# Float64 weights unpacked during the first layer and kept, split, in DRAM

## The chip, the cores and the metric

One core of a Trainium2 chip runs the kernel. The metric is device time in microseconds (us), the median over runs. Engines are called as in the profile: PE (TensorE, matmuls), PEld (its weight loads), DVE (VectorE), ACT (ScalarE), POOL (GpSimd), SP (SyncE, whose queue issues nearly all DMAs). L12 is line 12 of the kernel before.

## What is computed

A kernelized attention makes x (1152 tokens by 512). A first layer of four experts (512 to 1024 to 512, ReLU) is summed with token weights, and a second layer follows. Its weights arrive as float64.

```python
x = attention(q, k, v, omega)              # [1152, 512]
for e in range(4):                         # w1 [4, 512, 1024], w2 [4, 1024, 512], float32
    h = np.maximum(x @ w1[e], 0.0)
    out += p[:, e:e+1] * (h @ w2[e])
h = out @ w_in                             # w_in [512, 2048], float64
return ((h * np.cos(h)) @ w_out).astype(np.float32)   # w_out [2048, 512], float64
```

## The kernel before, in words

Every float32 product runs as three float32r products: an operand is split into hi and lo, and hi*hi, hi*lo and lo*hi are added. So each weight is needed as a hi tile and a lo tile.

The dense layers are six "experts": 0 to 3 are the first layer's, 4 and 5 the two halves of the second layer's 2048 hidden units. Each expert passes over three chunks of 384 tokens. A chunk has eight hidden tiles (`hidden`, L174, 12 matmuls each, 128x384), and three output tiles (`gemm2`, L220, 24 matmuls each, 128x512). Two hidden tiles of the next chunk run ahead of a chunk's second product (`gemm1_ahead`), so that on PE the order is 96 matmuls of L174, 72 of L220, 96 of L174, and so on.

The stream of dense work is cut into quanta (one hidden tile, or a third of an output tile); a chunk has 17 and an expert 51. Behind a quantum each side chain under way takes one step (`advance`), and `plan` says behind which quantum a chain starts. The order on each engine is thus the program's order; Tile adds the waits.

Evacuation of a hidden tile: in the first layer `relu_split`, one ACT and one DVE instruction (L230, L231). In the second layer `cos_split`, a chain of seven: ACT cv (L240), DVE ck (L241), POOL cv (L244), ACT ck (L246), DVE cv (L247), ACT hh (L249), DVE hl (L250). PE needs hh and hl of all eight tiles in each output tile, and the last of them near its end.

Weights come in sets (an expert's first or second product) of four units. Set number mod 3 picks one of three sets of buffers in SBUF. `load32` (first layer) takes a DMA, an ACT copy to hi and a DVE subtraction to lo (L96). `load64` (second layer) handles half a unit: a DMA of raw words (L110 or L118), ACT Abs (L122), five DVE instructions (L129, L132, L137, L140, L142), an ACT copy to hi (L145), and two POOL instructions, the subtraction (L147) and the addition of the low word to lo (L148). There are 32 such halves. `plan` starts them in expert 3 (sets 8 and 9) and expert 4 (sets 10 and 11), one expert ahead of their use. All raw tiles, of both kinds, share three buffers.

`second_x` turns the first layer's output back into the second's input: 12 groups of three transposes on PE (L298), four of them during the first chunk of expert 4.

Of the kernel before, what the change touches and what calls it, by code (L numbers as in the profile page):

```python
# [8 lines left out]
F32 = mybir.dt.float32  # L9
F32R = mybir.dt.float32r  # L10
# [5 lines left out]
# float32 products run as three float32r products: every operand is split exactly  # L16
# into hi (its 12 leading bits) and lo (the rest), and
# a*b = a_hi*b_hi + a_hi*b_lo + a_lo*b_hi up to 2**-24 of the product.

INV_2PI = 0.15915494309189535  # L20
TWO_PI_DOWN = 6.283185  # largest float32 whose half does not pass pi
# [4 lines left out]
def performer_moe_kernel(ctx, tc, q, k, v, omega, probs, w1, w2, w_in, w_out, out):  # L26
    nc = tc.nc
# [6 lines left out]
    R = 4  # neighbouring tokens in a partition  # L34
    SB = P * R  # tokens of a batch in whole tiles
    L = S - SB  # tokens of a batch in the shared tile
# [3 lines left out]
    TC = 3  # token tiles of a chunk  # L40
# [4 lines left out]
    EPS = 1e-6 * M  # the features are kept without their 1/sqrt(M)  # L45
# [11 lines left out]
    late = {}  # pools that take the attention's place  # L57
# [5 lines left out]
    # Set 2 * e is expert e's w1, set 2 * e + 1 its w2; the two halves of the second  # L63
    # layer's hidden units go as experts E and E + 1.
# [34 lines left out]
    def load64(st, u, z):  # L99
        """Half z of a unit, as three steps. float64 words are (low, high); the high word's  # L100
        21 bits make the float32 a, and the low word weighs 2**-52 times a's power of two."""
        hf = st // 2 - E
        n = UW // 2
        tmpp = late["tmp"]
        t = tmpp.tile([P, n], U32, tag="f64t", name=f"t{st}_{u}_{z}")
        raw = rawp.tile([P, n, 2], U32, tag="raw", name=f"raw{st}_{u}_{z}")
        lw, hw = raw[:, :, 0], raw[:, :, 1]
        if st % 2 == 0:
            c0 = hf * F + u * 256
            nc.sync.dma_start(  # L110
                out=raw.rearrange("p (k f) t -> p k f t", f=256),
                in_=w_in32[z * 256 : (z + 1) * 256, c0 : c0 + 256, :].rearrange(
                    "(k p) f t -> p k f t", p=P
                ),
            )
        else:
            r0 = hf * F + u * 256 + z * P
            nc.sync.dma_start(out=raw, in_=w_out32[r0 : r0 + P, :, :])  # L118
        yield
        yield  # L120
        # magnitudes below float32's range become 0
        nc.scalar.activation(t.bitcast(F32), hw.bitcast(F32), ACTF.Abs)  # L122
        yield
        if z == 0:
            new_unit(st, u)
        hi, lo = (x[:, z * n : (z + 1) * n] for x in units[st, u])
        a = tmpp.tile([P, n], U32, tag="f64a", name=f"a{st}_{u}_{z}")
        b = tmpp.tile([P, n], F32, tag="f64b", name=f"b{st}_{u}_{z}")
        nc.vector.tensor_scalar(  # L129
            out=t.bitcast(F32), in0=t.bitcast(F32), scalar1=2.0**-15, scalar2=None, op0=ALU.max  # L130
        )
        nc.vector.tensor_scalar(  # L132
            out=a, in0=t, scalar1=0x07FFFFFF, scalar2=3,
            op0=ALU.bitwise_and, op1=ALU.logical_shift_left,
        )
        yield
        nc.vector.scalar_tensor_tensor(  # L137
            out=a, in0=hw, scalar=0xC0000000, in1=a, op0=ALU.bitwise_and, op1=ALU.bitwise_or
        )
        nc.vector.tensor_scalar(out=t, in0=a, scalar1=0xFF800000, scalar2=None, op0=ALU.bitwise_and)  # L140
        yield
        nc.vector.scalar_tensor_tensor(  # L142
            out=b, in0=lw, scalar=2.0**-52, in1=t.bitcast(F32), op0=ALU.mult, op1=ALU.mult
        )
        nc.scalar.activation(hi, a.bitcast(F32), ACTF.Copy)  # L145
        yield
        nc.gpsimd.tensor_tensor(out=a.bitcast(F32), in0=a.bitcast(F32), in1=hi.bitcast(F32), op=ALU.subtract)  # L147
        nc.gpsimd.tensor_tensor(out=lo, in0=a.bitcast(F32), in1=b, op=ALU.add)  # L148
        yield

# [8 lines left out]
    def advance(under):  # L159
        """One step of each chain that is under way, the oldest first."""  # L160
        for g in list(under):
            if next(g, under) is under:
                under.remove(g)

    def hidden(e, c, f):
        """A tile of the hidden layer: [128 units, CW tokens]."""
        xh, xl = x_t[c]
        wh, wl = units[2 * e, f // 2]
        acc_ps = bank(f"g1_{e}_{c}_{f}")[:, :CW]
        n = 0  # L170
        for kk in range(KD):
            o = kk * 256 + (f % 2) * P
            for a, b_ in ((wh, xh), (wh, xl), (wl, xh)):
                nc.tensor.matmul(  # L174
                    acc_ps, a[:, o : o + P], b_[:, kk, :], start=n == 0, stop=n == 3 * KD - 1
                )
                n += 1
        return acc_ps

    heads = {}  # hidden tiles that run ahead, before the last chunk's second product  # L180
# [24 lines left out]
    def gemm2(e, c, evac):  # L205
        last = (e, c) == (E + 1, NCH - 1)
        for j in (2, 0, 1) if last else range(TC):
            # the very last tile in two pieces, so that less is left to do behind it
# [27 lines left out]
    def cos_split(src, hh, hl):  # L236
        vv = late["g"].tile([P, CW], F32, tag="cv", name="cv")
        kk = late["g"].tile([P, CW], F32, tag="ck", name="ck")
        # cos(h) = sin(2 pi (u - round(u))), u = h / (2 pi) + 1/4
# [51 lines left out]
    def second_x(c):  # L291
        """The first layer's output of a chunk as the second one's input, by steps."""
        new_x(c)
        xh, xl = x_t[c]
        for kk in range(KD):
            tp = bank(f"tx2_{c}_{kk}")[:, :CW]
            for j in range(TC):
                nc.tensor.transpose(  # L298
                    tp[:, j * P : (j + 1) * P], acc[c * TC + j][:, kk * P : (kk + 1) * P], ident
                )  # L300
            yield
            nc.scalar.activation(xh[:, kk, :], tp, ACTF.Copy)
            nc.vector.tensor_tensor(
                out=xl[:, kk, :], in0=tp, in1=xh[:, kk, :].bitcast(F32), op=ALU.subtract
            )

    # Expert e in quanta: chunk c begins at 17 * c with 6 of gemm1, 2 of the next chunk's
    # gemm1 and 9 of gemm2. starts[e][q]: what begins behind quantum q.
# [7 lines left out]
    def plan():  # L316
        for st in range(2, 2 * E + 4):
            e, k = st // 2 - 1, st % 2
            for u in range(NU):
                if st < 2 * E:  # L320
                    q = 38 + 3 * u if k else (20 + 4 * u if e == 0 else 3 + 9 * u)
                    start_at(e, q, lambda st=st, u=u: load32(st, u))
                else:
                    for z in range(2):
                        q = 30 + 2 * (2 * u + z) if k else 3 + 3 * (2 * u + z)
                        start_at(e, q, lambda st=st, u=u, z=z: load64(st, u, z))
# [5 lines left out]
    def dense():  # L332
# [3 lines left out]
        for n, (e, c) in enumerate(seq):  # L336
            if c == 0:
                q = 0
            parts = [gemm1(e, c, relu_split if e < E else cos_split)]
# [19 lines left out]
    with tc.tile_pool(name="at1", bufs=1) as at1, tc.tile_pool(name="at2", bufs=2) as at2:  # L359
        # work that wakes the tensor engine's clock while the first loads are under way  # L360
# [7 lines left out]
        # the table of exponentials comes in while the first loads are under way  # L368
# [5 lines left out]
        # values of the shared tile, each batch's rows in columns of their own  # L374
# [31 lines left out]
        # omega transposed, one copy for each half of a pair, the other half's rows zero  # L406
# [19 lines left out]
        def norms(nm, t):  # L426
            """sum((x * SC)**2) / 2 of each row."""
# [10 lines left out]
        def turn(nm, t):  # L438
            """Rows in pairs, transposed; what it returns splits them."""
# [14 lines left out]
        def features(nm, turned, phi):  # L454
            """phi[:, row, :] = exp(h - max(h)), h = SC * proj - sq; in three steps."""
# [18 lines left out]
            # max(h) = SC * max(proj) - sq, then the exponent's bias -sq - max(h)  # L474
# [17 lines left out]
        def divide(nm, parts):  # L492
            """dst = num / (den + eps) for (num, dst) in parts, 4 groups of D + 1 columns each."""
# [13 lines left out]
        def put_x(nm, kk, xs, t0, n):  # L507
            """Token tiles t0 .. t0 + n - 1 of the heads of pair kk into the chunks."""
# [19 lines left out]
        # per pair: [features, head, batch, value and count]  # L528
# [94 lines left out]
        # loads, two pairs ahead  # L623
# [22 lines left out]
        first = 6  # the step from which batch 0 is through  # L646
# [38 lines left out]
        # in the place of the first queries' features, which come after it  # L685
        xkL = at1.tile([P, 2, R * P], F32R, tag="phq", name="xkL")
        turned["kL"] = turn("kL", kL)(xkL[:, 0, :], xkL[:, 1, :])
        for s in range(NPR + 3):
# [14 lines left out]
            if s == 0:  # L703
                # the keys of the tile that both batches share
# [60 lines left out]
    late["tmp"] = ctx.enter_context(tc.tile_pool(name="tmp64", bufs=2))  # L765
    late["g"] = ctx.enter_context(tc.tile_pool(name="gp", bufs=3))
    new_acc(ctx.enter_context(tc.tile_pool(name="acc2", bufs=1)), TC, NTILE)
    for _ in stream:
        pass
# [28 lines left out]
```

## Time and profile before

| | |
|---|---|
| median of 3 runs | 721.22 us (720.83 to 721.45) |
| span of the profiled execution | 719.5 us |
| median less span (what lies around it) | 1.7 us |
| PE busy | 697.3 us, 97% of the span |
| DVE, ACT, POOL busy | 410.2, 250.9, 203.3 us |
| granted TensorE clock, mean | 0.991 |
| moved by DMA | 43.68 MB, mean 61 GB/s |

How to read it: the span is one execution, from first to last instruction. Busy matmuls overlap in the records, so a busy share of PE near 100% says that it never waited long, not that it was at its peak; a stage's length is therefore read from when its first matmul and the next stage's first matmul start.

### The profile page before, as it was taken

The numbers are of one execution on the slowest core, as the hardware profiler recorded it, in microseconds if no ns is written. First come the engines' busy times: TensorE is split into PE (matmuls) and PEld (weight loads), VectorE is DVE, ScalarE is ACT, GpSimd is POOL, SyncE is SP. The second block draws the span as 40 slices with busy tenths as digits, with TensorE's granted clock in tenths as the row PEclk, the third lists the DMA queues.
The fourth block names the chain that finished last, engine by engine and source line by source line (L and its number), as shares of the span: only waits on it lengthen the run. The fifth ranks groups of instructions, "written<-read, shape, count | busy, mean of one in ns | idle before, by whom it ended". The sixth has DMA issues, their size and how long they took to land.

```text
span 719.5 us, 9723 instructions
## 1 busy us (share of the span) xinstructions
PE 697.3 (97%) x3781; PEld 632.3 (88%) x3781; DVE 410.2 (57%) x755; ACT 250.9 (35%) x556; POOL 203.3 (28%) x168
## 2 busy tenths in 40 slices
PE   8999999999999999999999999999997998889998
PEld 8889998989898998989898989999786796769897
DVE  6999753414323232423133488599789889865252
ACT  4776740313121212112031223233645463253240
POOL 6565320000000000000000144345657566644150
PEclk9999999999999999999999999999999898999999
DMA  7554110022200011100022122123021212000001
GB/s 190 179 134 126 38 59 1 30 58 67 81 30 29 31 30 58 59 30 30 29 59 61 57 74 88 51 89 111 29 87 60 88 55 65 27 16 30 21 24 45
DMA packets 37519, 43.68 MB, mean 61 GB/s; under 512 B 13664, under 2 KB 26208, under 8 KB 37472
## 3 DMA queue, kind: packets, MB, share of 16 engines
q1 hardware_dynamic: 37328, 43.02, 20.0%
q8 instruction: 30, 0.49, 0.3%
q14 instruction: 17, 0.14, 0.1%
q10 hardware_dynamic: 144, 0.03, 0.0%
HBM read 40.68 MB, written 2.36 MB: 60 GB/s over the span
## 4 chain that ended last, share of the span: by engine, by line
PE 69%; DVE 20%; ACT 5%; issue 2%; POOL 1%; DMA 1%; SPq 0%; DVEq 0%; ACTq 0%
PE g L174 33%; PE g L220 31%; DVE t L129 3%; DVE a L132 2%; DVE hl L250 2%; DVE a L137 2%; DVE b L142 2%; DVE ck L241 1%; DVE cv L247 1%; ACT phk L487 1%; ACT hh L249 1%; PE num L577 1%; DVE mx_k L471 1%; PE pj_q L467 1%; PE kv L548 1%
## 5 line engine op out<-in xcount | busy, mean ns | idle before, releaser
L230 ACT ACTIVATE hh<-g 128x384 fp32r<-128x384 f32 x96 | 47.2, 493 | 255.7 <-PE g L174 154.0
L147 POOL TENSOR_TENSOR a<-a,w_0h 128x512 f32<-128x512 f32 x8 | 12.5, 1562 | 328.6 <-ACT w_0h L145 318.5
L231 DVE SCALAR_TENSOR_TENSOR hl<-g,hh 128x384 fp32r<-128x384 f32 x96 | 51.8, 554 | 83.3 <-ACT hh L230 83.2
L267 DVE SCALAR_TENSOR_TENSOR acc<-g,pn,acc 128x512 f32<-128x512 f32 x27 | 20.3, 750 | 102.2 <-PE g L220 102.2
L244 POOL TENSOR_TENSOR cv<-cv,ck 128x384 f32<-128x384 f32 x48 | 58.2, 1218 | 62.8 <-DVE ck L241 62.8
L174 PE MATMUL g<-xh,w_0h 128*128 128x384 f32 x144 | 48.9, 340 | 2.9 <-DVE cv L247 2.9
L174 PE MATMUL g<-xh,w_3h 128*128 128x384 f32 x144 | 48.7, 338 | 0.7 <-ACT acc L276 0.7
L220 PE MATMUL g<-w_2h,hl 128*128 128x512 f32 (+1 forms) x110 | 43.5, 396 | 5.9 <-DVE hl L250 5.9
L174 PE MATMUL g<-xh,w_2h 128*128 128x384 f32 x144 | 48.6, 337 | 0.0
L174 PE MATMUL g<-xh,w_1h 128*128 128x384 f32 x144 | 48.4, 336 | 0.0
L174 PE MATMUL g<-xh,w_1l 128*128 128x384 f32 x144 | 48.3, 336 | 0.0
L174 PE MATMUL g<-xl,w_1h 128*128 128x384 f32 x144 | 48.2, 335 | 0.0
L174 PE MATMUL g<-xh,w_3l 128*128 128x384 f32 x144 | 48.2, 335 | 0.0
L174 PE MATMUL g<-xh,w_0l 128*128 128x384 f32 x144 | 48.2, 335 | 0.0
L174 PE MATMUL g<-xl,w_0h 128*128 128x384 f32 x144 | 48.1, 334 | 0.0
L174 PE MATMUL g<-xh,w_2l 128*128 128x384 f32 x144 | 48.1, 334 | 0.0
L174 PE MATMUL g<-xl,w_3h 128*128 128x384 f32 x144 | 48.1, 334 | 0.0
L174 PE MATMUL g<-xl,w_2h 128*128 128x384 f32 x144 | 48.1, 334 | 0.0
L220 PE MATMUL g<-w_3h,hh 128*128 128x512 f32 (+1 forms) x110 | 44.4, 404 | 2.4 <-ACT hh L249 2.4
L220 PE MATMUL g<-w_2h,hh 128*128 128x512 f32 (+1 forms) x110 | 43.1, 392 | 2.1 <-ACT hh L249 2.1
L220 PE MATMUL g<-w_3h,hl 128*128 128x512 f32 (+1 forms) x110 | 43.8, 398 | 0.0
L220 PE MATMUL g<-w_0h,hl 128*128 128x512 f32 (+1 forms) x110 | 43.4, 395 | 0.0
(187 smaller groups left out, 1839.5 us busy)
## 6 DMA issues: line engine op xcount, KB each, us to landing
raw<-in_moe_w_dram SPq DMA_DIRECT2D x32, 512.0 KB, 3.5
raw<-in_moe_w_in_dram SPq DMA_DIRECT2D x16, 512.0 KB, 3.7
raw<-in_moe_w_out_dram SPq DMA_DIRECT2D x16, 512.0 KB, 3.5
kt<-in_k_dram SPq DMA_DIRECT2D x8, 256.0 KB, 2.9
qt<-in_q_dram SPq DMA_DIRECT2D x8, 256.0 KB, 3.2
ve<-in_v_dram SPq DMA_DIRECT2D x16, 128.0 KB, 3.1
out_dram<-acc SPq DMA_DIRECT2D x7, 256.0 KB, 2.3
out_dram<-acc SPq DMA_DIRECT2D x4, 128.0 KB, 2.3
```

The costliest lines, as they stand in the source:

```text
L129: nc.vector.tensor_scalar(out=t.bitcast(F32), in0=t.bitcast(F32), scalar1=2.0**-15, scalar2=None, op0=ALU.max)
L132: nc.vector.tensor_scalar(out=a, in0=t, scalar1=0x07FFFFFF, scalar2=3, op0=ALU.bitwise_and, op1=ALU.logical_shift_left,)
L137: nc.vector.scalar_tensor_tensor(out=a, in0=hw, scalar=0xC0000000, in1=a, op0=ALU.bitwise_and, op1=ALU.bitwise_or)
L142: nc.vector.scalar_tensor_tensor(out=b, in0=lw, scalar=2.0**-52, in1=t.bitcast(F32), op0=ALU.mult, op1=ALU.mult)
L147: nc.gpsimd.tensor_tensor(out=a.bitcast(F32), in0=a.bitcast(F32), in1=hi.bitcast(F32), op=ALU.subtract)
L174: nc.tensor.matmul(acc_ps, a[:, o : o + P], b_[:, kk, :], start=n == 0, stop=n == 3 * KD - 1)
L220: nc.tensor.matmul(acc_ps, a[:, cs], b_[:, ws], start=n == 0, stop=n == 3 * FT - 1)
L230: nc.scalar.activation(hh, src, ACTF.Relu)
L231: nc.vector.scalar_tensor_tensor(out=hl, in0=src, scalar=0.0, in1=hh.bitcast(F32), op0=ALU.max, op1=ALU.subtract)
L244: nc.gpsimd.tensor_tensor(out=vv, in0=vv, in1=kk, op=ALU.subtract)
L250: nc.vector.tensor_tensor(out=hl, in0=vv, in1=hh.bitcast(F32), op=ALU.subtract)
L267: nc.vector.scalar_tensor_tensor(out=acc[t], in0=src, scalar=p_, in1=acc[t], op0=ALU.mult, op1=ALU.add)
```

## The change

`load64` becomes `convert64`. It makes hi and lo in temporary tiles rather than in the weight buffers, its last two instructions (subtraction and addition) move from POOL to DVE, the ACT copy to hi goes ahead of the DVE product in program order, and two DMAs on SP's queue write hi and lo (256 KB each) to a DRAM scratch. A new `load64` reads a whole unit back: two DMAs of 512 KB into the weight buffers. The 32 conversions start every fifth quantum, from quantum 16 of expert 0 to quantum 18 of expert 3. The loads of sets 8, 9, 10 and 11 start at quantum 3 of expert 3, 42 of expert 3, 1 of expert 4 and 42 of expert 4, a unit a quantum. The pool of the conversion's temporaries is closed where expert 4 begins, and the cosine's tiles (`gp`) then take its place.

```diff
+    dram = ctx.enter_context(tc.tile_pool(name="dram", bufs=1, space=bass.MemoryType.DRAM))
+    kept = {}
-    def load64(st, u, z):
+    def convert64(st, u, z):
...
+        if (st, u) not in kept:
+            kept[st, u] = tuple(
+                dram.tile([P, UW], F32, tag=f"k{st}_{u}{s}", name=f"k{st}_{u}{s}") for s in "hl"
+            )
...
-        if z == 0:
-            new_unit(st, u)
-        hi, lo = (x[:, z * n : (z + 1) * n] for x in units[st, u])
...
+        hi = tmpp.tile([P, n], F32R, tag="f64h", name=f"h{st}_{u}_{z}")
+        lo = tmpp.tile([P, n], F32R, tag="f64l", name=f"l{st}_{u}_{z}")
...
+        nc.scalar.activation(hi, a.bitcast(F32), ACTF.Copy)
         nc.vector.scalar_tensor_tensor(
             out=b, in0=lw, scalar=2.0**-52, in1=t.bitcast(F32), op0=ALU.mult, op1=ALU.mult
         )
-        nc.scalar.activation(hi, a.bitcast(F32), ACTF.Copy)
-        yield
-        nc.gpsimd.tensor_tensor(out=a.bitcast(F32), in0=a.bitcast(F32), in1=hi.bitcast(F32), op=ALU.subtract)
-        nc.gpsimd.tensor_tensor(out=lo, in0=a.bitcast(F32), in1=b, op=ALU.add)
-        yield
+        yield
+        nc.vector.tensor_tensor(out=a.bitcast(F32), in0=a.bitcast(F32), in1=hi.bitcast(F32), op=ALU.subtract)
+        nc.vector.tensor_tensor(out=lo, in0=a.bitcast(F32), in1=b, op=ALU.add)
+        for part, dst in zip((hi, lo), kept[st, u]):
+            nc.sync.dma_start(out=dst[:, z * n : (z + 1) * n], in_=part.bitcast(F32))
+        yield
+
+    def load64(st, u):
+        for dst, src in zip(new_unit(st, u), kept[st, u]):
+            nc.sync.dma_start(out=dst.bitcast(F32), in_=src)
+        yield
...
-        for st in range(2, 2 * E + 4):
+        for st in range(2, 2 * E):
...
-                else:
-                    for z in range(2):
-                        q = 30 + 2 * (2 * u + z) if k else 3 + 3 * (2 * u + z)
-                        start_at(e, q, lambda st=st, u=u, z=z: load64(st, u, z))
+        for i in range(4 * 2 * NU):
+            st, u, z = 2 * E + i // (2 * NU), i % (2 * NU) // 2, i % 2
+            start_at(0, 16 + 5 * i, lambda st=st, u=u, z=z: convert64(st, u, z))
+        for st, e, q in ((2 * E, E - 1, 3), (2 * E + 1, E - 1, 42), (2 * E + 2, E, 1), (2 * E + 3, E, 42)):
+            for u in range(NU):
+                start_at(e, q + u, lambda st=st, u=u: load64(st, u))
...
+            if (e, c) == (E, 0):
+                late["closing"].close()
+                late["g"] = ctx.enter_context(tc.tile_pool(name="gp", bufs=3))
...
-    late["tmp"] = ctx.enter_context(tc.tile_pool(name="tmp64", bufs=2))
-    late["g"] = ctx.enter_context(tc.tile_pool(name="gp", bufs=3))
     new_acc(ctx.enter_context(tc.tile_pool(name="acc2", bufs=1)), TC, NTILE)
+    late["closing"] = ctx.enter_context(ExitStack())
+    late["tmp"] = late["closing"].enter_context(tc.tile_pool(name="tmp64", bufs=2))
```

## Rows read from the trace of the kernel before

**Rows 1.** The page's first part: busy us, share of the span, instructions.

```profile
PE 697.3 (97%) x3781; PEld 632.3 (88%) x3781; DVE 410.2 (57%) x755; ACT 250.9 (35%) x556; POOL 203.3 (28%) x168
```

**Rows 2.** The page's second part: POOL's busy tenths in 40 slices of 18 us.

```profile
DVE  6999753414323232423133488599789889865252
...
POOL 6565320000000000000000144345657566644150
```

**Rows 3.** Windows cut at first matmuls of stages: length, busy (instructions), PEclk, DMA share, GB/s.

```profile
core 0: us, PE busy (x) PEld busy (x) DVE busy (x) ACT busy (x) POOL busy (x), PEclk, DMA share, GB/s
...
425.28:443.34 18.06, 18.06 (x110) 17.93 (x108) 15.70 (x27) 7.83 (x16) 7.34 (x5) 1.00 0.22 66
494.14:511.78 17.64, 17.14 (x98) 16.63 (x96) 15.16 (x22) 7.53 (x15) 11.09 (x9) 1.00 0.27 87
511.78:532.38 20.60, 19.36 (x85) 14.32 (x85) 18.55 (x31) 11.25 (x24) 10.81 (x8) 1.00 0.15 44
...
549.05:573.35 24.30, 20.32 (x73) 14.62 (x73) 21.93 (x31) 10.76 (x22) 14.29 (x11) 0.86 0.21 67
...
590.02:613.46 23.44, 20.14 (x74) 15.12 (x73) 21.64 (x28) 8.52 (x16) 14.67 (x11) 0.85 0.28 90
613.46:633.93 20.47, 17.38 (x97) 16.56 (x96) 17.46 (x24) 8.49 (x18) 13.24 (x10) 1.00 0.00 0
633.93:653.83 19.90, 18.03 (x73) 13.12 (x73) 8.36 (x17) 6.61 (x15) 5.26 (x4) 1.00 0.07 28
653.83:670.50 16.67, 16.67 (x98) 16.67 (x97) 11.84 (x24) 9.81 (x22) 9.95 (x8) 1.00 0.05 17
670.50:686.86 16.36, 16.36 (x74) 13.51 (x73) 1.94 (x3) 0.94 (x3) 0.00 (x0) 1.00 0.08 32
```

**Rows 4.** Windows again: the disturbed stretch whole, and the first layer.

```profile
494.14:653.83 159.69, 145.71 (x685) 123.70 (x684) 132.30 (x193) 71.79 (x146) 91.42 (x69) 0.96 0.18 56
128.20:425.28 297.08, 297.08 (x1514) 271.44 (x1512) 100.17 (x140) 62.57 (x103) 8.78 (x6) 1.00 0.16 48
```

**Rows 5.** Who PE waited for from 494 to 654: us, times, longest us.

```profile
PE g L220 <- DVE hl L250: 5.9, 3, 2.9
PE g L220 <- ACT hh L249: 4.5, 11, 0.5
PE g L174 <- DVE cv L247: 2.9, 2, 2.4
```

**Rows 6.** DVE in order of time: start us, us, instruction; the first conversion.

```profile
405.48 0.56 DVE L231 SCALAR_TENSOR_TENSOR hl<-g,hh 128x384 fp32r<-128x384 f32 x1 [1.52 <-ACT hh L230]
406.03 0.43 DVE L129 TENSOR_SCALAR t<-t 128x512 f32<-128x512 f32 x1
...
406.96 0.69 DVE L137 SCALAR_TENSOR_TENSOR a<-raw,a 128x512 uint32<-128x512 uint32 x1
407.68 0.43 DVE L140 TENSOR_SCALAR t<-a 128x512 uint32<-128x512 uint32 x1
408.14 0.69 DVE L142 SCALAR_TENSOR_TENSOR b<-raw,t 128x512 f32<-128x512 uint32 x1
...
410.31 1.40 DVE L132 TENSOR_SCALAR a<-t 128x512 uint32<-128x512 uint32 x1
```

**Rows 7.** POOL in order of time, the same stretch.

```profile
410.07 1.35 POOL L148 TENSOR_TENSOR w_0l<-a,b 128x512 fp32r<-128x512 f32 x1
```

**Rows 8.** DVE by line, 113 to 400 us: busy us, mean ns.

```profile
L96 DVE TENSOR_TENSOR w_0l<-raw,w_0h 128x1024 fp32r<-128x1024 f32 x6 | 7.3, 1222 | 1.6 <-ACT w_0h L93 1.6
```

**Rows 9.** ACT by line from 400 us on: busy us, mean ns.

```profile
L122 ACT ACTIVATE t<-raw 128x512 f32<-128x512 f32 x32 | 21.3, 664 | 7.0 <-DVE b L142 6.8 <-DMA raw<-in_moe_w_out_dram 0.2
```

**Rows 10.** DVE in order of time: a chunk's last hidden tile, no conversion near.

```profile
670.71 0.56 DVE L250 TENSOR_TENSOR hl<-cv,hh 128x384 fp32r<-128x384 f32 x1 [0.59 <-ACT hh L249]
```

**Rows 11.** DMA issues: KB each, median us from issue to landing.

```profile
raw<-in_moe_w_in_dram SPq DMA_DIRECT2D x16, 512.0 KB, 3.7
```

**Rows 12.** Windows of 10 us: the stretch with most bytes moved.

```profile
10.00:20.00 10.00, 9.53 (x81) 9.30 (x80) 9.69 (x30) 6.86 (x25) 5.97 (x7) 1.00 0.78 216
```

More of the change, by code (lines that the diff above doesn't have):

```diff
@@ L316, in plan @@
     def plan():
-        for st in range(2, 2 * E + 4):
+        for st in range(2, 2 * E):
             e, k = st // 2 - 1, st % 2
             for u in range(NU):
-                if st < 2 * E:
-                    q = 38 + 3 * u if k else (20 + 4 * u if e == 0 else 3 + 9 * u)
-                    start_at(e, q, lambda st=st, u=u: load32(st, u))
-                else:
-                    for z in range(2):
-                        q = 30 + 2 * (2 * u + z) if k else 3 + 3 * (2 * u + z)
-                        start_at(e, q, lambda st=st, u=u, z=z: load64(st, u, z))
+                q = 38 + 3 * u if k else (20 + 4 * u if e == 0 else 3 + 9 * u)
+                start_at(e, q, lambda st=st, u=u: load32(st, u))
+        for i in range(4 * 2 * NU):
[4 more added lines that the diff above has]
+                start_at(e, q + u, lambda st=st, u=u: load64(st, u))
         for c, q in enumerate((18, 36, QE + 8)):
```

## The prediction

> **What bounds the kernel now.** I read the page's busy times first, then its slices, then windows cut at the stages, then who PE waited for. PE is busy 97% of the span and no other engine above 57% [rows 1]. So only time in which PE does not run at its pace can be won, and the busy share does not show where that is. DVE is busy 100.17 of 297.08 us in the first layer, a third, but 132.30 of 159.69, 83%, from 494 to 654 us [rows 4], and POOL, idle since slice 7, is back at work from slice 23 [rows 2]: the stretch where the float64 halves are unpacked beside the cosine chain.
>
> The windows turn this into a price. An undisturbed chunk is 96 matmuls of the first product in 16.67 us and 72 of the second in 16.36 us, 33.03 us together (the last two of [rows 3]). With four groups of transposes in it a stage grows by 18.06 - 16.67 = 1.39 us [rows 3]. From 494.14 to 653.83 there are four of each product and four groups of transposes: 4 x 33.03 + 1.39 = 133.51 us at the undisturbed pace, and the stretch took 159.69 [rows 4]. The excess is 26.2 us. By stages: the first chunk's first product 17.64 - 16.67 = 1.0 and second 20.60 - 16.36 - 1.39 = 2.9; the second and third chunks' second products 24.30 - 16.36 = 7.9 and 23.44 - 16.36 = 7.1; in expert 5 20.47 - 16.67 = 3.8 and 19.90 - 16.36 = 3.5 [rows 3]. Together 26.2, so the two stages not shown lost nothing. In the first layer, 128.20 to 425.28, nine chunks took 297.08 = 9 x 33.01 us [rows 4]: nothing is lost there, nor after 653.83.
>
> PE's own waits in the stretch name the cosine chain's ends, hl, hh and cv, but sum to only some 14 us [rows 5]. The rest I read as pace behind such waits: the granted clock averages 0.86 and 0.85 in the two worst stages, 1.00 in the others [rows 3]. All of it begins with a late evacuation, and the evacuations are late because DVE is full: 21.93 of 24.30 and 21.64 of 23.44 us busy [rows 3].
>
> **What the change removes.** Nothing of experts 4 and 5 but the cosine chain, `second_x` and the output remains on DVE, ACT and POOL. What that looks like is in the trace: the second chunk of expert 5 has the same chain and no conversion, and runs at 16.67 and 16.36 us with DVE at 11.84 of 16.67 [rows 3]. Its last hidden tile has hl at 670.71 + 0.56 = 671.27 us [rows 10]; that tile is first needed 21 of 72 matmuls into the second product, 670.50 + 21/72 x 16.36 = 675.27. The chain is 4.0 us early, so no wait is next in line behind the one removed. The first chunk of expert 4 has four steps of `second_x` besides, each an ACT copy and a DVE subtraction of a size that takes about 0.56 us [rows 6], and they come behind the last evacuation in program order. I take the whole 26.2 us as gone; if chunk one of expert 4 kept its excess, 1.0 + 2.9 = 3.9 us would stay.
>
> **What it adds on DVE.** Without POOL beside it, L129 and L140 take 0.43 us and L137 and L142 0.69 [rows 6]. L132 took 1.40 us while POOL ran L148 [rows 6, 7]; in the first layer POOL is idle [rows 2], so I take L129's 0.43, with 1.40 as the upper bound. The two moved instructions (two tensors, 128x512) are not in the trace on DVE: between 0.56 (384 wide, L231) [rows 6] and 1.22 (1024 wide, L96) [rows 8]; I take L137's 0.69. A conversion is 3 x 0.43 + 4 x 0.69 = 4.05 us, at most 6.08 with both upper bounds. Thirty-two are 130 us (195 at most), spread over some 161 quanta of 33.03/17 = 1.94 us, that is 313 us: 41% (62%). DVE is at 100.17/297.08 = 34% there [rows 4], so 75%, and 96% at the upper bound.
>
> Is there cover? A conversion's heaviest step is 1.38 us, two chains can meet in a quantum, and a `load32` subtraction adds 1.22 [rows 8]: about 4 us of work ahead of an evacuation at worst. In a first-layer chunk the last hl ended at 405.48 + 0.56 = 406.04 [rows 6]; its second product began at 425.28 - 16.36 = 408.92 [rows 3] and needs it at 408.92 + 4.77 = 413.69. So 7.6 us of lag on DVE or ACT cost PE nothing. I price this at nothing; without that cover each conversion could cost up to its 4 us.
>
> **ACT and SP.** ACT keeps its two instructions, about 0.66 us each [rows 9]: 32 x 1.3 = 42 us moved into a stretch where ACT is busy 62.57 of 297.08 us [rows 4]. SP gets 64 writes and 32 loads more. A write waits on SP for DVE's lo, and the next raw loads queue behind it; before, SP could issue a raw load as soon as a buffer came free. A conversion's raw load comes one quantum before the previous conversion's writes, so it stands behind writes that are about four quanta old. A `load32` that starts in the quantum of a write is worse off: lo about 2 us late, 3.7 to land [rows 11], against two quanta (3.9 us) until ACT reads it. ACT then stands for about 2 us, with its next hh behind it and DVE behind that; inside the 7.6 us, so nothing on PE.
>
> **The loads.** A set is 8 x 512 KB = 4.19 MB. Sets 9 and 11 are tight: issued behind quantum 42 and needed by the next expert's quantum 8, 16 quanta or 31 us later, the last unit 4 us after that. One after the other they take 8 x 3.7 = 30 us [rows 11]; at the most the trace moved, 216 GB/s [rows 12], 19. Both fit; I take 19. Sets 8 and 10 have over twice the time.
>
> The Trainium skill (SBUF — State Buffer, section The DMA setup-cost knee) gives a transfer as about 2 us plus its bytes at 436 GB/s, which would bring a set in within some 12 us, an estimate. The trace bears out the fixed part (a 512 KB load would take 3.2 us by it, the row has 3.7 [rows 11]) but shows no such rate, 216 GB/s being its most [rows 12]. By either the sum is the same.
>
> **The sum.** 719.5 - 26.2 = 693.3 us of span; the median shown lies 1.7 us above the profiled span, so 695.0 us. Allowing 0.5 for the odd short wait, 695.5.
>
> **The rivals.**
> 1. Part of the excess stays or comes back: the first cosine chunk is late by itself (3.9 us, above), or the first layer loses some at each expert's busiest place, where a `load32` wave, a raw buffer not yet free and two conversions meet. For it: DVE at 75% with 96% at the bound. Against it: 7.6 us of slack. Four such places at 2 us give 8; with the 3.9, 12. Time 698 to 707.
> 2. The loads come late: against it the 19 to 30 us above. Each us that sets 9 and 11 are late costs two; late by 5 us, 705. Even the serial bound fits, and in the second layer SP has little else to issue.
> 3. Slower: DVE becomes the first layer's bound. At 6.08 us a conversion DVE is at 96%, bunching then exceeds the slack in the first product's stages, and each of 32 conversions must cost PE 26.2/32 = 0.82 us for the gain to be eaten. At 1.5 us each the time would be 695 + 48 = 743. It needs POOL's disturbance without POOL, so I hold it unlikely.
>
> **How the numbers follow.** Forecast (694 to 697.5): 0.70. Rival 1: 0.18. Rival 2: 0.06. Rival 3: 0.04, and 0.02 for about no change. The predicted time is the likeliest one's, 695.5. Low end 693.5: the undisturbed pace less the runs' scatter. High end 703: it takes in half of rival 1. A measurement tells some 0.2% (1.4 us) from no change: faster 0.94, same 0.02, slower 0.04.
>
> **What would show it.** The stages of experts 4 and 5 at 16.67 and 16.36 us, with a granted clock of 1.00; DVE near 75% in the first layer and the moved instructions near 0.69 us; no wait of PE for hh or hl in the first layer; the reads of a set landed well before the next expert's second product. The prediction is wrong if first-layer stages grow, if a cosine stage stays above 16.67, or if PE waits for a load of the scratch.

## The result, and the profile after

The changed kernel takes 694.29 us (694.1 to 694.31, four runs) against 721.34 (720.83 to 721.54): a ratio of 0.9628, 95% interval 0.9615 to 0.9642. The forecast was 695.5, with 693.5 to 703.0. The profiled execution's span is 692.5 us, PE is busy 684.4 of it, and the mean granted clock is 1.0 where it was 0.991.

Windows of the changed kernel over stages of experts 4 and 5, in the columns of [rows 3]: length, busy us (instructions) of PE, PEld, DVE, ACT and POOL, granted clock, DMA share, GB/s. Each cut lies some 0.16 us, one matmul, behind the stage's first matmul, so the lengths hold.

```profile
493.41:510.07 16.66, 16.66 (x98) 16.66 (x97) 12.85 (x24) 9.97 (x22) 9.48 (x8) 1.00 0.48 186
510.07:527.88 17.81, 17.81 (x86) 14.66 (x85) 2.69 (x5) 3.03 (x7) 0.00 (x0) 1.00 0.00 1
...
544.54:560.90 16.36, 16.36 (x74) 13.51 (x73) 0.56 (x1) 1.22 (x3) 0.00 (x0) 1.00 0.17 64
577.57:593.93 16.36, 16.36 (x73) 13.51 (x73) 0.56 (x1) 1.22 (x3) 0.00 (x0) 1.00 0.01 2
593.93:610.60 16.67, 16.67 (x98) 16.67 (x97) 11.40 (x23) 11.38 (x26) 9.97 (x8) 1.00 0.00 0
610.60:626.96 16.36, 16.36 (x73) 13.51 (x73) 1.94 (x3) 0.78 (x3) 0.00 (x0) 1.00 0.09 33
```

These are the six stages that were too long in [rows 3]: 17.64, 20.60, 24.30, 23.44, 20.47 and 19.90 us have become 16.66, 17.81 (with four groups of transposes), 16.36, 16.36, 16.67 and 16.36. In the second products DVE's busy time went from 21.93 and 21.64 us to 0.56.

The two long stretches of [rows 4] in the changed kernel, same columns:

```profile
127.31:424.55 297.24, 297.24 (x1514) 271.60 (x1513) 198.49 (x333) 92.36 (x156) 0.00 (x0) 1.00 0.48 159
493.41:626.96 133.55, 133.55 (x686) 121.86 (x685) 52.83 (x103) 50.32 (x109) 39.41 (x32) 1.00 0.16 59
```

The stretch that took 159.69 us takes 133.54 from first matmul to first matmul (493.25 to 626.79; 133.55 by the cuts shown); its undisturbed length had been worked out as 133.51. The first layer took on 98 us of DVE work (198.49 for 100.17) and 30 of ACT and is no longer than before: 297.24 us from first matmul to first matmul in both kernels. (The 297.08 of [rows 4] begins one matmul late, at 128.20 for 128.04.) The span's 27.0 us are thus 26.15 from this stretch and 0.89 from the start, since the first layer's stretch begins at 127.15 rather than 128.04; what lies behind 626.79 is 0.04 longer. I take the 0.89 for scatter of the start: in the run below in which the two POOL instructions move to DVE in place, whose first change comes at the first conversion, behind 400 us, the same stretch begins at 127.02.

Who PE waited for in the changed kernel, the whole list: us in total, times, longest us.

```profile
PE tp_q L462 <- DVE pT L586: 1.8, 4, 0.5
PE warm L385 <- DVE one L390: 1.1, 1, 1.1
PE tp_kL L462 <- DMA kL<-in_k_dram: 1.0, 1, 1.0
PE kvL L556 <- DVE xTl_q L469: 0.6, 1, 0.6
PE tq L581 <- ACT phq L507: 0.3, 1, 0.3
```

All five are in the attention. The hl, hh and cv of [rows 5] are gone, and no other wait took their place: from the first dense chunk on PE waits for nothing.

DVE by line (busy us, mean ns): three of the conversion's lines, the second a moved one.

```profile
L144 DVE SCALAR_TENSOR_TENSOR a<-raw,a 128x512 uint32<-128x512 uint32 x32 | 22.0, 688 | 0.5
...
L154 DVE TENSOR_TENSOR a<-a,h 128x512 f32<-128x512 f32 x32 | 21.9, 683 | 0.0
...
L139 DVE TENSOR_SCALAR a<-t 128x512 uint32<-128x512 uint32 x32 | 13.7, 428 | 1.1
```

The seven instructions of a conversion have means of 420, 428, 688, 427, 685, 683 and 692 ns: 4.02 us, where 4.05 was forecast.

### The profile page after: what moved, and what is told of

It reads as the page before. It is cut to its first block, busy times and chain, and to the rows that moved or that the text cites. A ratio compares the mean times of both kernels' runs of the same rounds, so it can differ in the third digit from the quotient of the medians.

```text
span 692.5 us, 9782 instructions
## 1 busy us (share of the span) xinstructions
PE 684.4 (99%) x3781; PEld 629.5 (91%) x3781; DVE 396.9 (57%) x819; ACT 249.8 (36%) x556; POOL 112.3 (16%) x104
## 4 chain that ended last, share of the span: by engine, by line
PE 91%; DVE 5%; ACT 2%; DMA 1%; issue 0%; SPq 0%
PE g L189 43%; PE g L235 43%; ACT phk L507 1%; PE num L597 1%; DVE mx_k L491 1%; PE pj_q L487 1%; PE kv L568 1%; DMA kL<-in_k_dram 1%; PE tx L313 1%; PE tq L581 1%; DVE mx_k L496 0%; PE pj_k L487 0%; DVE sq_k L455 0%; DMA qt<-in_q_dram 0%; DVE xs L523 0%
## 5 line engine op out<-in xcount | busy, mean ns | idle before, releaser
L256 DVE TENSOR_SCALAR ck<-cv 128x384 f32<-128x384 f32 x48 | 18.8, 397 | 50.0 <-ACT cv L255 47.5
L261 ACT ACTIVATE ck<-cv 128x384 f32<-128x384 f32 x48 | 24.6, 513 | 56.1 <-POOL cv L259 56.1
L235 PE MATMUL g<-w_1h,hh 128*128 128x512 f32 (+1 forms) x110 | 42.6, 388 | 0.0
L235 PE MATMUL g<-w_0l,hh 128*128 128x512 f32 (+1 forms) x110 | 42.6, 387 | 0.0
L235 PE MATMUL g<-w_1l,hh 128*128 128x512 f32 (+1 forms) x110 | 42.5, 386 | 0.0
```

The source lines that it names most:

```text
L235: nc.tensor.matmul(acc_ps, a[:, cs], b_[:, ws], start=n == 0, stop=n == 3 * FT - 1)
L256: nc.vector.tensor_scalar(out=kk, in0=vv, scalar1=ROUND, scalar2=ROUND, op0=ALU.add, op1=ALU.subtract)
L261: nc.scalar.activation(kk, vv, ACTF.Sin, scale=TWO_PI_DOWN)
```

## The experiments

The theory was that the 26 us were lost because the unpacking shares DVE (and POOL) with the cosine chain in expert 4, and that the first layer has slack enough to take it. Two questions stand against it: which part of the unpacking cost what, and how much the first layer can take. Each run is compared with the kernel before on the same chip. In all of them the first-layer stages kept 16.66 and 16.36 us, except where the text says otherwise.

### Half of the sets at a time

Sets 10 and 11 alone early and through DRAM, sets 8 and 9 unpacked in expert 3 by the old code (`unpack64`, the old `load64`):

```diff
-        for i in range(4 * 2 * NU):
-            st, u, z = 2 * E + i // (2 * NU), i % (2 * NU) // 2, i % 2
+        for st in (2 * E, 2 * E + 1):
...
+                    q = 30 + 2 * (2 * u + z) if st % 2 else 3 + 3 * (2 * u + z)
+                    start_at(E - 1, q, lambda st=st, u=u, z=z: unpack64(st, u, z))
+        for i in range(2 * 2 * NU):
+            st, u, z = 2 * E + 2 + i // (2 * NU), i % (2 * NU) // 2, i % 2
             start_at(0, 16 + 5 * i, lambda st=st, u=u, z=z: convert64(st, u, z))
...
```

> Sets 10 and 11 alone are converted in the first layer and go through DRAM; sets 8 and 9 are unpacked in expert 3 as before. Theory (the 26 us were lost where the cosine chain shares DVE with the unpacking, and expert 3 has no cosine chain): nearly all of the gain, 694 to 697 us; 1 us may stay at the start of expert 4, where set 9's last halves end. Rival (each half converted early brings its share): half of the gain, about 708 us.

Measured: 699.14 us, ratio 0.9703 (0.9688 to 0.9717). The mirror image, sets 8 and 9 early and sets 10 and 11 unpacked in expert 4:

```diff
-        for i in range(4 * 2 * NU):
+        for i in range(2 * 2 * NU):
             st, u, z = 2 * E + i // (2 * NU), i % (2 * NU) // 2, i % 2
             start_at(0, 16 + 5 * i, lambda st=st, u=u, z=z: convert64(st, u, z))
...
+        for st in (2 * E + 2, 2 * E + 3):
...
+                    q = 30 + 2 * (2 * u + z) if st % 2 else 3 + 3 * (2 * u + z)
+                    start_at(E, q, lambda st=st, u=u, z=z: unpack64(st, u, z))
...
```

> The mirror image: sets 8 and 9 are converted early and go through DRAM, sets 10 and 11 are unpacked in expert 4 beside the cosine chain as before. Theory: next to nothing gained, 718 to 721 us (at most the 1.0 us of expert 4's first stage and a little of the next). Rival of equal shares: about 708 us.

Measured: 712.66 us, ratio 0.9885 (0.9869 to 0.9902). Neither theory nor rival holds in either run: the late half alone gains 22 us and the early half alone 8.4, and I had expected next to nothing of the early one. The windows say where its 8.4 us come from. With sets 10 and 11 early, expert 4's first two stages stay long:

```profile
493.30:512.00 18.70, 17.09 (x98) 16.57 (x96) 13.78 (x22) 7.64 (x15) 11.12 (x9) 1.00 0.44 166
512.00:532.60 20.60, 19.36 (x86) 14.33 (x85) 9.00 (x18) 8.66 (x19) 5.28 (x4) 1.00 0.00 1
532.60:549.30 16.70, 16.70 (x98) 16.70 (x97) 11.41 (x23) 11.25 (x25) 9.99 (x8) 1.00 0.01 1
```

With sets 8 and 9 early these two are clean, and the later four are long:

```profile
544.50:565.00 20.50, 18.93 (x74) 14.52 (x74) 18.15 (x24) 7.37 (x14) 12.66 (x10) 0.92 0.30 81
...
581.60:605.00 23.40, 20.10 (x73) 15.36 (x73) 21.60 (x28) 8.47 (x16) 14.48 (x10) 0.85 0.27 91
605.00:625.30 20.30, 17.45 (x97) 16.58 (x97) 17.30 (x24) 8.48 (x18) 13.23 (x10) 1.00 0.00 0
625.30:645.20 19.90, 18.05 (x74) 13.16 (x73) 8.38 (x17) 6.61 (x15) 5.27 (x4) 1.00 0.07 28
```

So set 9 is at fault in the first two stages: it is planned for expert 3, and its end runs over into expert 4. The kernel before shows it on DVE in order of time, 7 us after PE began the next expert's stage at 494.14:

```profile
501.35 0.43 DVE L140 TENSOR_SCALAR t<-a 128x512 uint32<-128x512 uint32 x1
501.81 0.69 DVE L142 SCALAR_TENSOR_TENSOR b<-raw,t 128x512 f32<-128x512 uint32 x1
502.42 0.75 DVE L267 SCALAR_TENSOR_TENSOR acc<-g,pn,acc 128x512 f32<-128x512 f32 x1
503.08 2.17 DVE L241 TENSOR_SCALAR ck<-cv 128x384 f32<-128x384 f32 x2
```

The first two cosine tiles (L241) stand behind that. The delay isn't DVE's alone. ACT waits 4.4 us for DVE before its last copy to hi (at 501.35), with the cosine's cv right behind it (501.88), and POOL's first cosine step (504.98) stands behind that conversion's two instructions. And the delay travels: the second chunk's second product took 24.30 us in [rows 3] and 20.5 with sets 8 and 9 early. The test of it leaves only set 8 behind:

```diff
-        for i in range(4 * 2 * NU):
-            st, u, z = 2 * E + i // (2 * NU), i % (2 * NU) // 2, i % 2
+        for u in range(NU):
+            for z in range(2):
+                start_at(E - 1, 3 + 3 * (2 * u + z), lambda u=u, z=z: unpack64(2 * E, u, z))
+        for i in range(3 * 2 * NU):
+            st, u, z = 2 * E + 1 + i // (2 * NU), i % (2 * NU) // 2, i % 2
             start_at(0, 16 + 5 * i, lambda st=st, u=u, z=z: convert64(st, u, z))
...
```

> Sets 9, 10 and 11 are converted early and go through DRAM; set 8 is unpacked at the beginning of expert 3 as before. Theory (what stayed where sets 10 and 11 alone went early was set 9's backlog on DVE, which reaches into expert 4): the whole gain, 694 to 695 us. Rival (unpacking in expert 3 costs by itself, whichever set): set 8 keeps some 2 us or more, 696 to 699 us.

Measured: 694.39 us, ratio 0.9629 (0.9615 to 0.9644), all stages clean. So set 8 costs nothing. Sets 10 and 11 cost 18.4 us when they alone are left late (712.66 against 694.29). Set 9's spill costs 4.9 when it alone is left (699.14), and some 8 with sets 10 and 11 behind it, to which it passes its delay on: the two costs don't simply add.

### Which engine, or when

The kernel before with only the two POOL instructions moved to DVE:

```diff
-        nc.gpsimd.tensor_tensor(out=a.bitcast(F32), in0=a.bitcast(F32), in1=hi.bitcast(F32), op=ALU.subtract)
-        nc.gpsimd.tensor_tensor(out=lo, in0=a.bitcast(F32), in1=b, op=ALU.add)
+        nc.vector.tensor_tensor(out=a.bitcast(F32), in0=a.bitcast(F32), in1=hi.bitcast(F32), op=ALU.subtract)
+        nc.vector.tensor_tensor(out=lo, in0=a.bitcast(F32), in1=b, op=ALU.add)
```

> The kernel before with one edit: the subtraction and the addition of a conversion run on DVE instead of POOL; nothing moves in time, nothing goes through DRAM. Theory (DVE is full in expert 4, and its time for a conversion stays near 4.1 us, since two more instructions of 0.69 replace what the others lost beside POOL): little change, 712 to 722 us. Rival (POOL's two instructions, which make DVE's 0.43 us ones take 1.35, are the cause): most of the gain without any scratch, 695 to 702 us.

Measured: 705.65 us, ratio 0.9788 (0.9773 to 0.9803). Again between theory and rival: more than half of the gain (15.4 of 27) with no scratch and nothing moved in time. Its windows: the first cosine chunk is clean, and three stages are still long.

```profile
544.20:564.70 20.50, 18.95 (x75) 14.53 (x74) 18.06 (x35) 7.54 (x15) 2.52 (x2) 0.92 0.34 102
...
581.30:602.30 21.00, 18.77 (x74) 14.47 (x73) 19.17 (x38) 8.22 (x16) 2.52 (x2) 0.92 0.35 101
...
619.00:638.40 19.40, 17.83 (x73) 13.10 (x73) 7.88 (x16) 6.26 (x14) 4.87 (x4) 1.00 0.07 28
```

DVE by line in that stretch shows how two more instructions can leave DVE no fuller:

```profile
L132 DVE TENSOR_SCALAR a<-t 128x512 uint32<-128x512 uint32 x17 | 7.3, 427 | 0.6
...
L129 DVE TENSOR_SCALAR t<-t 128x512 f32<-128x512 f32 x17 | 7.1, 420 | 0.0
```

L132 took 1145 ns and L129 1082 in the kernel before from 494 to 654 us. The five instructions added up to 4.36 us there; seven now take about 4.1, POOL has only the cosine's step left, and the unpacking is no longer a chain over three engines. DVE is about as busy as before in the two worst stages (18.06 of 20.50 and 19.17 of 21.00 us), and yet they lose 4.1 and 4.6 us rather than 7.9 and 7.1: how full DVE is doesn't by itself set the loss. The opposite edit, the changed kernel with the two instructions back on POOL:

```diff
-        nc.vector.tensor_tensor(out=a.bitcast(F32), in0=a.bitcast(F32), in1=hi.bitcast(F32), op=ALU.subtract)
-        nc.vector.tensor_tensor(out=lo, in0=a.bitcast(F32), in1=b, op=ALU.add)
+        nc.gpsimd.tensor_tensor(out=a.bitcast(F32), in0=a.bitcast(F32), in1=hi.bitcast(F32), op=ALU.subtract)
+        nc.gpsimd.tensor_tensor(out=lo, in0=a.bitcast(F32), in1=b, op=ALU.add)
```

> The changed kernel with the two instructions back on POOL: only the time of the conversions and the way through DRAM differ from the kernel before. Theory (time alone matters): 694 to 695 us, with DVE's share in the first layer near the changed kernel's since its instructions lengthen beside POOL, and still no wait of PE. Rival (POOL beside DVE is what delays evacuations): first-layer stages over 16.67 and 16.36 us, 698 us or more.

Measured: 694.16 us, ratio 0.9631 (0.9616 to 0.9645). The first layer in one window, 179.30 us of DVE and 92.83 of POOL:

```profile
126.90:424.20 297.30, 297.30 (x1514) 271.62 (x1513) 179.30 (x273) 91.96 (x156) 92.83 (x60) 1.00 0.48 159
```

Here the engine makes no difference: it matters only beside the cosine chain. Of the change's two parts the move in time is enough by itself; the move to DVE is not needed once the time is moved, and alone is worth 15 us.

### DVE and POOL apart, and together

Idle work was added to expert 4 of the changed kernel, in the quanta of the old conversions: their two POOL instructions on a scratch tile, their five DVE instructions on scratch tiles, and both. The edit with both (the other two leave out the lines of one engine; the one with POOL alone reads a second scratch tile; the scratch tiles and their first filling are cut here):

```diff
+    def extra():
...
+        nc.vector.tensor_scalar(
+            out=dt.bitcast(F32), in0=dt.bitcast(F32), scalar1=2.0**-15, scalar2=None, op0=ALU.max
+        )
...
+        yield
+        nc.gpsimd.tensor_tensor(out=dp, in0=dp, in1=dp, op=ALU.subtract)
+        nc.gpsimd.tensor_tensor(out=dp, in0=dp, in1=dp, op=ALU.add)
+        yield
...
+        for i in range(2 * 2 * NU):
+            start_at(E, 30 + 2 * (i - 2 * NU) if i >= 2 * NU else 3 + 3 * i, extra)
```

> The changed kernel with idle work added in expert 4: sixteen pairs of POOL instructions (subtract and add of a scratch tile, 128x512) in the quanta where the kernel before has its conversions' pairs, with nothing else of a conversion. Theory A (POOL hurts by filling DVE: DVE's instructions lengthen beside it, but without the conversions' own DVE work there is room): 694 to 696 us. Theory B (POOL's queue delays the cosine chain's own POOL step, which stands behind 2.9 us of other work): 698 to 708 us.

> The changed kernel with idle work added in expert 4: a conversion's five DVE instructions on scratch tiles, sixteen times, in the quanta of the kernel before; no POOL work, no ACT work. Theory A (DVE's total decides; 2.7 us unlengthened beside a cosine chain of 1.5 us a tile is about 80% of DVE): 694 to 698 us. Theory B (POOL's queue alone is the cause): 694 to 695 us. More than 700 us would say that DVE's queue alone explains most of the 26 us.

> The idle DVE work and the idle POOL work of the last two runs together, sixteen times in expert 4 of the changed kernel: DVE and POOL as in the kernel before, but no link between them, no ACT work and no raw words. Apart they cost 1.0 and 1.9 us. Theory (DVE and POOL hold one another up, and together they fill both): well over the sum, 703 to 713 us, the latter being what sets 10 and 11 unpacked there cost. Rival (the sum holds, and what cost 18 us was the conversion's chain through ACT and the waits on raw words): 697 to 699 us.

Measured, in that order: 696.2 us, ratio 0.9654 (0.9638 to 0.967); 695.25 us, ratio 0.9642 (0.9628 to 0.9656); and 707.91 us, ratio 0.9828 (0.9809 to 0.9847). Against 694.29 these are 1.9, 1.0 and 13.6 us. The first lies just above theory A's 694 to 696 and below theory B's 698 to 708, so POOL's queue alone doesn't explain the loss; nor does DVE's own work. Together they cost over four times the sum, without any link between the two, any ACT work or raw words. Who PE waited for from the dense chunks on, in the run with both:

```profile
PE g L263 <- DVE hl L293: 3.8, 5, 1.9
PE g L263 <- ACT hh L292: 2.6, 6, 0.5
```

And DVE by line over its experts 4 and 5 up to the last disturbed stage:

```profile
L293 DVE TENSOR_TENSOR hl<-cv,hh 128x384 fp32r<-128x384 f32 x39 | 29.3, 751 | 7.3 <-ACT hh L292 6.9
...
L177 DVE TENSOR_SCALAR da<-dt 128x512 uint32<-128x512 uint32 x16 | 10.4, 652 | 0.6
L174 DVE TENSOR_SCALAR dt<-dt 128x512 f32<-128x512 f32 x16 | 9.8, 612 | 0.4
```

The releasers are hl and hh as in [rows 5], and the lines lengthen here too, though less than in the kernel before: L177 to 652 ns from 427 with DVE's work alone, L174 to 612 from 470. The real halves cost 18.4 us (712.66 less 694.29), so some 5 us of it are not in this imitation. Whether they come from the links between the engines or from DVE's instructions, which lengthen more there, stays open. The links are a real candidate: with sets 10 and 11 late, POOL stands 27 us (494 to 645 us) at the subtraction for ACT's hi, with the cosine's steps behind it.

### How much the first layer can take

The product b of each conversion issued several times:

```diff
-        nc.vector.scalar_tensor_tensor(
-            out=b, in0=lw, scalar=2.0**-52, in1=t.bitcast(F32), op0=ALU.mult, op1=ALU.mult
-        )
+        for _ in range(4):
+            nc.vector.scalar_tensor_tensor(
+                out=b, in0=lw, scalar=2.0**-52, in1=t.bitcast(F32), op0=ALU.mult, op1=ALU.mult
+            )
```

> The changed kernel with the product b of each conversion issued four times on DVE, the same product into the same tile: 4.02 + 3 x 0.69 = 6.1 us of DVE a conversion, which is the prediction's upper bound, and 96% of DVE in the first layer. Theory (lag stays inside the 7.6 us of slack as long as DVE's load is under 100%): 694 to 699 us. Rival 3 of the prediction (at that price bunching exceeds the slack and each conversion costs PE 0.8 us or more): 720 us or more.

Measured: 694.3 us, ratio 0.9627 (0.9613 to 0.9641), as if nothing had been added. The first layer's window:

```profile
127.20:424.50 297.30, 297.30 (x1514) 271.62 (x1514) 253.77 (x420) 92.25 (x156) 0.00 (x0) 1.00 0.47 159
```

DVE is at 253.77 of 297.30, 85% (the 96% expected did not come), and PE runs at its pace. With `range(6)`:

> The same with the product six times: 4.02 + 5 x 0.69 = 7.5 us of DVE a conversion, 110% of DVE. Theory: DVE becomes the first layer's bound; about 10% of 313 us, some 30 us, less the slack of 7.6 once: 715 to 727 us. Rival (conversions only wait for one another and the evacuations pass them, so PE is not held): 694 to 697 us.

Measured: 733.23 us, ratio 1.0163 (1.0144 to 1.0181): slower than the kernel before, by 39 us against the changed one, more than the 21 to 33 expected. First-product stages of the first layer grow to as much as 28 us. One of them, and PE's longest wait in it in order of time:

```profile
195.30:221.70 26.40, 19.47 (x98) 19.15 (x97) 21.11 (x35) 7.25 (x14) 0.00 (x0) 0.81 0.40 134
```

```profile
212.81 0.69 PE L190 MATMUL g<-xh,w_3h 128*128 128x384 f32 x1 [6.93 <-DVE acc L279]
```

What runs out here is not the slack of the evacuations but PSUM: PE is about to go on with a hidden tile and waits 6.9 us for a bank that an output tile's evacuation, late in DVE's queue, still holds. The granted clock averages 0.81 in that stage; what that adds to the loss wasn't separated. Nor is DVE simply full: it is busy 21.11 of 26.40 us, less than the 85% above. ACT stands 7.1 us at a `load32`'s raw words there (to 205.54), with five evacuations behind it and DVE behind ACT. So the late raw loads have a part in it that no run separates from DVE's load. That the first layer can be lost this way, as rival 3 of the prediction feared, is real; the edge lies between 6.1 and 7.5 us of DVE a conversion, and the change is at 4.0.

The slack itself, with fewer tiles running ahead:

```diff
-    AHEAD = 2
+    AHEAD = 0
```

> The changed kernel without the two hidden tiles that run ahead of a chunk's second product (AHEAD 0 for 2): the slack behind a chunk's last evacuation falls by 4.17 us, to 3.4 us in the first layer and to -0.2 in the second. Theory (this slack is what hides the conversions and the cosine chain): the first layer still loses little or nothing, six cosine chunks lose a few tenths of a us each plus a restart, 695 to 699 us. Rival (the conversions' bunching and ACT's waits for raw words need more than 3.4 us): first-layer stages grow, 703 us or more.

> The changed kernel with one tile ahead: slack 5.5 us in the first layer, 1.9 in the second. Theory: still all hidden, 694 to 695 us. Rival (bunching needs more): 697 us or more.

Measured: 694.3 us, ratio 0.9626 (0.961 to 0.9642), with none ahead, and 694.38, ratio 0.9626 (0.9612 to 0.9641), with one. With none I had worked out a slack of -0.2 us in the cosine chunks, and a loss of a few us. The trace shows my error. A chunk's last hl on DVE, and PE's matmuls that read the last hidden tile, with none ahead:

```profile
610.65 0.56 DVE L265 TENSOR_TENSOR hl<-cv,hh 128x384 fp32r<-128x384 f32 x1 [0.59 <-ACT hh L264]
```

```profile
611.08 0.39 PE L235 MATMUL g<-w_3h,hh 128*128 128x512 f32 x1
611.30 0.39 PE L235 MATMUL g<-w_3l,hh 128*128 128x512 f32 x1
611.53 0.39 PE L235 MATMUL g<-w_3h,hl 128*128 128x512 f32 x1
```

hl ends at 611.21, after the tile's first matmul has begun; but hl is read by the third, at 611.53. For hl the slack is 0.45 us more than I had counted, and 0.3 us of it is left here. The first layer, with 3.4 us by the same count, lost nothing either.

## Why the prediction was right

**The excess and its place.** The 26.2 us worked out from stage lengths came back as 26.15, and the stages named are those that shrank. This step carried the forecast: it needs no cause, only a stage of the same kind that runs undisturbed. The forecast came out 1.2 us too long: the 0.5 allowed for the odd wait wasn't needed, and the start's 0.89 is scatter that no sum could hold.

**Where PE lost it.** PE idled 14.0 us in the stretch (159.69 less 145.71): the waits of [rows 5] and 0.7 us more. The other 12.2 are busy time, 145.71 us for 133.54, and the prediction put them down to the granted clock. At most 7.7 of them can be: that is what the two stages at 0.86 and 0.85 have too much (20.32 and 20.14 for 16.36). The other 4.4 lie in stages at 1.00. PE's weight loads (PEld) waited 24.9 us for hh, hl, cv and acc in the stretch, a row that the prediction did not read and that comes near the excess by itself.

**The cause.** "The evacuations are late because DVE is full" named one part of two; the number did not depend on it, and that is why it came out. The imitation shows that DVE's work alone costs 1.0 us and POOL's alone 1.9, and both together 13.6; moving POOL's part to DVE in place gains 15 us. The prediction saw that instructions lengthen beside POOL [rows 6, 7], but priced it only for the first layer. The Trainium skill (SBUF — State Buffer, section Who interferes with whom) says that some VectorE instructions share a pair of SBUF ports with GpSimd, and that whichever begins first holds the pair for its whole instruction while the other waits. The trace agrees: in [rows 6, 7] L132 ends at 411.71, 0.29 us behind the L148 that began before it (411.42). Whether it is this, POOL's queue or the waits between the engines that makes the two together so dear, no run separates.

**The first cosine chunk.** Rival 1 held that its 3.9 us might be its own. They were set 9's spill (with sets 8 and 9 early both stages are clean), and are gone.

**The cost on DVE.** 4.02 us a conversion for 4.05. DVE's share of the first layer came out at 67% rather than 75%, in part because the 34% taken for the rest [rows 4] already held the first conversions of the kernel before, which begin at 406 us [rows 6].

**The cover.** Right, and larger than said: 6.1 us a conversion cost nothing, where the prediction let rival 3 begin, and DVE was then at 85%, not 96. For hl the slack is 0.45 us longer than worked out.

**ACT and SP.** This step was mis-sized. ACT was to stand for about 2 us at a raw load now and then; these are its longest waits of that kind in the changed kernel, from 127 to 440 us:

```profile
ACT w_3h L93 <- DMA raw<-in_moe_w_dram: 25.3, 5, 8.3
...
ACT w_1h L93 <- DMA raw<-in_moe_w_dram: 18.8, 3, 8.7
ACT t L130 <- DMA raw<-in_moe_w_out_dram: 17.2, 3, 11.1
```

That is up to 11.1 us at a time. Behind the waits of 8 us stands SP's queue, which waits at the scratch writes (L157) for ACT's h and DVE's l:

```profile
SPq L157 <- ACT h L149: 159.1, 28, 21.6
...
SPq L157 <- DVE l L155: 73.7, 28, 5.5
```

SP stands 233 us in all at the scratch writes, with raw loads queued behind: those that ended ACT's waits of 8.3, 8.7 and 8.1 us left within 0.5 us of such a write (at 157.43, 218.63 and 355.61). The longest wait, to 418.60, is another matter. Its raw load left at 407.73 and took 10.9 us to land, behind six of set 8's 512 KB loads that had left since 404.8; the DMA engines moved 413 GB/s from 412 to 416 us, nearly twice the 216 that the prediction took for the most. So the change's own loads queue against the raw words, which the prediction left out.

It cost nothing: the last hl of each of the nine first-layer chunks in the stretch still ends 7.6 us before its need. In part that is luck, since 11.1 us is more than the 7.6 of cover. The wait fell almost wholly into a second product (408.03 to 424.39), where the evacuations run on DVE and ACT has none to make.

**The loads.** On time, and earlier than forecast: SP doesn't wait for quantum 42. Set 9's eight loads left between 443.5 and 472.8 us, behind the last scratch write and as PE finished with each unit's buffer, for a need at 509.9. Issued in a burst, as set 10's were, a set's loads took up to 7.2 us (median of the last) where a 512 KB load took 3.7 in the kernel before [rows 11]. Rival 2 had nothing to work on.

## What to carry to other kernels

Price a stall by the length of a stage of the same kind that runs undisturbed, not by PE's booked waits alone: here 14 us of them were 26 us of stage (the weight loads' waits, 24.9 us, came nearer). Work that doesn't depend on the stage that it disturbs is worth moving, even by way of DRAM and back (33.6 MB more here), into a stage whose bottleneck has slack against it; first work out that slack in us at the point of use, and what else queues behind the moved waits and loads. And before a large move, try the small edits apart: taking two instructions off POOL gave more than half of this gain in two lines.

## What the hardware showed that I had not expected

Work on DVE and on POOL that cost 1.0 and 1.9 us apart cost 13.6 together. A DVE instruction of 0.43 us can take three times as long beside POOL: L132 averaged 1145 ns where the unpacking ran beside the cosine chain. In the first layer with POOL back at work, DVE at 60%, it was mostly other instructions that lengthened (the product b to 867 ns from 685), and PE lost nothing. And an engine at 85% busy, fed through ACT waits of up to 10.5 us, can leave the bottleneck's pace untouched to within 0.1 us, while two more products of 0.69 us a conversion (7.5 us for 6.1) cost 39 us.
